# The product W3·Wout inside a fused attention and MoE kernel: third matrix loaded transposed, contraction outside, four row blocks in four banks, the last unit's sums in one piece

## The chip, the cores and the metric

One core of one Trainium2 chip runs the whole program. The metric is the device time of one execution in microseconds; the time before is a median of three runs. Engines are named as the profile names them: PE (TensorE, with PEld for its weight loads), DVE (VectorE), ACT (ScalarE), POOL (GpSimd), SP (SyncE, which issues nearly all DMAs).

## The reference

```python
def _attn_ref(q, k, v, w1, b1, w2):            # 8 batches, 8 heads, 576 positions, 64 wide
   scores = q @ k^T / 8 + bias(i, j)           # bias: a small MLP of the relative position
   attn = exp(scores - max) / sum
   return attn @ v

def _moe_ref(x, w1, w2, w3, w_out):            # x: 4608 x 512; w1, w2: 512 x 1024
   a = x @ w1
   b = x @ w2
   h = a * b @ w3                              # w3: 1024 x 1024
   return (h @ w_out).astype(np.float32)       # w_out: 1024 x 512
```

`x` is the attention's output, 4608 tokens by 512. The four MoE matrices arrive as 64-bit floats.

## The kernel before

**Two stages with a seam.** The attention runs over 32 units (4 pairs of heads by 8 batches). Then the MoE part runs over 9 chunks of 512 tokens. Between them lies the seam, which the change is about: the kernel uses (a·b)·W3·Wout = (a·b)·(W3·Wout), so it computes the 1024 x 512 product W3·Wout once ("folding") and the MoE stage needs only `up` (both products with w1 and w2) and `down` (one product with the folded matrix).

**Order.** Every step of every engine has a planned time, in microseconds of the plan: `arrange` writes those of the attention, `put` and `put_w` those of the seam and the MoE part. `drive` hands the steps over in the order of the planned times, and the program is then built from them; PE, DVE, ACT and POOL each run their instructions strictly in the order in which they stand there. The order rows below show what was built. The plan's times are no measured times.

**One attention unit.** S: scores, 9 row tiles named `0246M1357`, each into one of two 2-bank buffers `ps_s`. T (DVE): adds the bias `nb` and finds the row minimum `mx`. E (ACT): the exponentials, into `pp`, with row sums into `sums`. R (DVE): transposes a pair of tiles into `pt`. W0 to W7 (PE, line 352): the products of `pt` with v, all into `acc`, four banks. X (ACT): copies `acc` into `x`, which goes to DRAM as `x_d`. Step `r` inverts the row sums and sends them out. A unit's W pieces stand among the S of the unit behind it; the last unit has none behind it.

**64-bit weights.** A matrix piece of 128 x 512 is fetched as 512 KB into `wi`, of which there are two buffers, and turned into 32-bit floats by two ACT, four DVE and two POOL steps (`narrow`, lines 140 to 164): `wmag` and the low part on ACT, clamp on POOL or DVE, shift, head and power on DVE, two POOL steps for the total. The 24 pieces of w3 and w_out are done during the attention, in `wos` and `w3s`. The 16 pieces of w1 and w2 are done in the seam and during the first `up` steps (`split_w`, clamps on DVE); the fetch of a piece waits until POOL has done with the piece two before it.

**Two-part numbers.** Each factor of a product is split into a high part (ACT, names with h) and a low part, the difference (DVE or POOL, names with l), and three PE matmuls are issued for each product: high·high, high·low, low·high.

**The seam before.** `split_wo(i)` splits the 8 row blocks of w_out: `woh` on ACT, `wol` on POOL (even i) or DVE (odd i). `fold(ft, hf)`, 16 calls, goes over the 8 row blocks ft of w3 and the two halves of its columns: 4 PE transposes into `w3t` (line 561), `w3h` on ACT (565) and `w3l` on DVE (567), both out of PSUM, then 12 matmuls of 128 x 512 into `wacc` (573), which holds one row block of the result. After the second half, two steps put the high and the low part of that row block into SBUF (579 on ACT, 581 on DVE). Buffers for `w3h` and `w3l`: two each. `w3t` takes one bank, `wacc` two banks in turn.

**The MoE stage.** `up(c, ft)`: 24 matmuls (614), then a, g, gh, gl on ACT and DVE. `down(c, ft)`: 12 matmuls (639) into four accumulators, one step behind. PE order at the start: up, up, down, up, down, and so on. The tokens of a chunk are loaded as `xr`, multiplied by the inverted sums `rb`, and split into `xh` (POOL) and `xl` (DVE).

Of the kernel before, what the change touches and what calls it, by code (L numbers as in the profile page):

```python
# [78 lines left out]
def relpos_attention_moe(  # L79
# [477 lines left out]
    def fold(ft, hf):  # L557
        ts = range(hf * NF // 2, (hf + 1) * NF // 2)
        tp = pst.tile([P, NF // 2, P], F32, name="w3t")
        for n, t in enumerate(ts):  # L560
            nc.tensor.transpose(tp[:, n], w3s[ft][:, t * P:(t + 1) * P], ident)  # L561
        yield
        w3h = fp.tile([P, NF // 2, P], F32R, name="w3h")
        w3l = fp.tile([P, NF // 2, P], F32R, name="w3l")
        nc.scalar.activation(w3h, tp, AF.Copy)
        yield
        nc.vector.tensor_tensor(w3l, tp, f(w3h), op=ALU.subtract)
        yield
        if hf == 0:
            wacc[ft] = psw.tile([P, DO], F32, name="wacc")  # L570
        for n, t in enumerate(ts):
            for m, (l, r) in enumerate(((w3h, woh), (w3h, wol), (w3l, woh))):
                nc.tensor.matmul(  # L573
                    wacc[ft], l[:, n], r[t], start=(t == 0 and m == 0), stop=(t == NF - 1 and m == 2),
                )
        yield
        if hf == 1:
            w = held.tile([P, 2, DO], F32R, name=f"w3s{ft}")
            nc.scalar.activation(w[:, 0], wacc[ft], AF.Copy)
            yield  # L580
            nc.vector.tensor_tensor(w[:, 1], wacc[ft], f(w[:, 0]), op=ALU.subtract)
            folded[ft] = w
# [48 lines left out]
    def down(c, ft):  # L631
        d = chunks[c]
        gh, gl = d["g"].pop(ft)
        for t in range(NT):
# [3 lines left out]
            for n, (l, r) in enumerate(((gh, 0), (gh, 1), (gl, 0))):  # L638
                nc.tensor.matmul(  # L639
                    d["o", t], l[:, sl], folded[ft][:, r],  # L640
# [11 lines left out]
    for i in range(NF):  # L652
        put(later, split_wo(i), t_s + AT_WO + i * PACE_WO, t_s + AT_WO + i * PACE_WO + 0.8)
    for i in range(2 * NF):
        at = t_s + AT_F + min(i, N_F) * PACE_F0 + max(i - N_F, 0) * PACE_F
        put(later, fold(*divmod(i, 2)), *(at + d for d in AT_FOLD))
    for t in range(2):
        for m in range(2):
            put_w(later, w01, t, m, t_s + AT_W1 + PACE_W * (2 * t + m))
# [84 lines left out]
```

## Time and profile before

| | |
|---|---|
| time before, median of 3 runs | 1181.52 us (1175.22 to 1184.53) |
| the profiled execution | 1180.03 us, span 1178.2 us, granted PE clock 0.981 |
| busy | PE 1112.6, PEld 771.2, DVE 686.3, ACT 484.1, POOL 181.2 us |
| last score tile's reduction starts (DVE, line 270) | 513.25 us |
| first and last fold matmul start (PE, line 573) | 519.5 and 584.7 us |
| first `down` matmul starts (PE, line 639) | 594.5 us |

The seam lies between 513 and 595 us. A line with "idle before" says how long the engine waited ahead of its instructions and what ended that wait. Line numbers are those of the kernel before.

### The profile page before, as it was taken

What the parts mean: (1) busy time and instruction counts of PE and PEld (TensorE: products, weight loads), DVE (VectorE), ACT (ScalarE), POOL (GpSimd) and SP (SyncE); (2) the same over time, 40 slices, a digit from 0 to 9 for tenths busy, and PEclk for the clock granted to TensorE, in tenths of its full rate; (3) what the DMA queues carried; (4) which work ended last, traced back from release to release, by engine and by line L of the source; (5) the groups of instructions that cost most, each with busy time, mean ns of one, the idle gap of its engine ahead of it and who ended that gap; (6) DMA issues with size and microseconds to landing.
All of it is one profiled execution on the core that took longest, in us unless ns stands there. A gap on an engine that the chain in (4) does not pass through costs nothing.

```text
span 1178.2 us, 34156 instructions
## 1 busy us (share of the span) xinstructions
PE 1112.6 (94%) x14720; PEld 771.2 (65%) x14720; DVE 686.3 (58%) x1284; ACT 484.1 (41%) x1071; POOL 181.2 (15%) x152
## 2 busy tenths in 40 slices
PE   7769989998899999898999999999999999999998
PEld 3225445444444554466888888888888888888887
DVE  8779988998899999986885222223131222223111
ACT  6756655665566666664442212121211212121212
POOL 0003320321033123333543000000000000000000
PEclk9979999999999999998999999999999999999999
DMA  8887786767776766636431211202010211100000
GB/s 261 279 261 229 231 285 206 242 214 244 234 234 222 237 222 205 217 120 173 132 117 54 72 36 54 54 36 72 35 55 19 72 36 56 52 36 1 36 1 36
DMA packets 91959, 158.51 MB, mean 135 GB/s; under 512 B 18336, under 2 KB 32800, under 8 KB 91808
## 3 DMA queue, kind: packets, MB, share of 16 engines
q1 hardware_dynamic: 91376, 156.31, 41.6%
q8 instruction: 115, 1.88, 0.6%
q14 instruction: 36, 0.29, 0.1%
q10 hardware_dynamic: 432, 0.02, 0.0%
HBM read 126.36 MB, written 29.92 MB: 133 GB/s over the span
## 4 chain that ended last, share of the span: by engine, by line
PE 68%; DVE 19%; issue 5%; DMA 5%; ACT 2%; SPq 0%; DVEq 0%; POOL 0%; ACTq 0%; POOLq 0%
PE up L614 33%; PE o L639 17%; PE acc L352 8%; DVE ts L270 8%; DVE pt L309 7%; PE s L259 6%; PE wacc L573 3%; DMA nb_d<-bev 2%; DMA v<-in_v_dram 1%; PE bacc L473 1%; DVE wmag L155 1%; ACT pp L299 1%; DVE wi L160 1%; DVE zdve L459 1%; PE w3t L561 0%
## 5 line engine op out<-in xcount | busy, mean ns | idle before, releaser
L352 PE MATMUL acc<-pt,v 32*64 32x128 f32 (+1 forms) x9216 | 245.0, 298 | 21.9 <-issue 12.2
L352 PEld LDWEIGHTS acc<-pt,v 32*64 32x64 f32 x9216 | 158.2, 133 | 145.0 <-issue 110.7
L622 DVE TENSOR_TENSOR g<-up,a 128x512 f32<-128x512 f32 x72 | 49.8, 691 | 342.8 <-PE up L614 342.8
L299 ACT ACTIVATE pp<-ts,mx 128x576 f32<-128x576 f32 x256 | 196.5, 769 | 95.0 <-DVE mx L270 93.9
L259 PE MATMUL s<-k,q 64*64 64x288 f32 x2304 | 208.8, 442 | 21.2 <-DVE mx L270 16.0
L614 PE MATMUL up<-xl,wh 128*128 128x512 f32 x576 | 225.1, 391 | 0.0
L614 PE MATMUL up<-xh,wl 128*128 128x512 f32 x576 | 225.1, 391 | 0.0
L614 PE MATMUL up<-xh,wh 128*128 128x512 f32 x576 | 225.1, 391 | 0.0
L270 DVE CUSTOM_DVE_ANT_0 ts<-s,nb 128x576 f32<-128x576 f32 x256 | 184.9, 745 | 41.1 <-PE s L259 28.2
L639 PE MATMUL o<-w3s,gh 128*128 128x512 f32 x576 | 177.7, 390 | 0.0
L309 DVE STREAM_TRANSPOSE pt<-pp 128x1152 f32<-128x1152 f32 x128 | 175.5, 1371 | 0.1
L619 ACT COPY a<-up 128x512 f32<-128x512 f32 x72 | 42.3, 587 | 257.7 <-PE up L614 257.7
L259 PEld LDWEIGHTS s<-k,q 64*64 64x64 f32 x2304 | 63.3, 135 | 97.8 <-issue 48.1
L614 PEld LDWEIGHTS up<-xh,wl 128*128 128x128 f32 x576 | 108.2, 188 | 23.4
L614 PEld LDWEIGHTS up<-xl,wh 128*128 128x128 f32 x576 | 108.2, 188 | 23.4
L614 PEld LDWEIGHTS up<-xh,wh 128*128 128x128 f32 x576 | 108.2, 188 | 23.3
L639 PEld LDWEIGHTS o<-w3s,gh 128*128 128x128 f32 x576 | 108.1, 188 | 22.9
L625 ACT ACTIVATE gh<-g 128x512 fp32r<-128x512 f32 x72 | 45.5, 633 | 178.3 <-DVE g L622 178.3
L639 PE MATMUL o<-w3s,gl 128*128 128x512 f32 x288 | 112.1, 389 | 0.0
L600 POOL TENSOR_SCALAR xh<-xr 128x512 fp32r<-128x512 f32 x36 | 23.2, 645 | 443.3 <-DVE xr L596 443.3
L628 DVE TENSOR_TENSOR gl<-g,gh 128x512 fp32r<-128x512 f32 x72 | 51.6, 717 | 50.7 <-ACT gh L625 50.5
L146 POOL TENSOR_SCALAR wmag<-wmag 128x512 f32<-128x512 f32 x24 | 46.0, 1915 | 207.9 <-ACT wmag L140 174.0
(67 smaller groups left out, 937.3 us busy)
## 6 DMA issues: line engine op xcount, KB each, us to landing
v<-in_v_dram SPq DMA_DIRECT2D x64, 320.0 KB
k<-in_k_dram SPq DMA_DIRECT2D x64, 288.0 KB
q<-in_q_dram SPq DMA_DIRECT2D x64, 288.0 KB
v<-in_v_dram SPq DMA_DIRECT2D x64, 256.0 KB
wi<-in_moe_w_dram SPq DMA_DIRECT2D x32, 512.0 KB
nb_d<-bev SPq DMA_DIRECT2D x36, 295.5 KB
nb<-nb_d SPq DMA_DIRECT2D x16, 576.0 KB
x_d<-x SPq DMA_DIRECT2D x32, 288.0 KB
```

The source lines that it names most:

```text
L146: clamps.tensor_scalar(d["mag"], d["mag"], LEAST, MOST, op0=ALU.max, op1=ALU.min)
L259: nc.tensor.matmul(s[outs, hf, :HS], d[f"q{h}"][rows, q0:q0 + 64], d[f"k{h}"][rows, hf * HS:(hf + 1) * HS], start=True, stop=True,)
L270: nc.vector.tensor_tensor_reduce(out=halves(ts), in0=d.pop(("s", t))[:, :, :HS], in1=halves(NB[p, t]), op0=ALU.add, op1=ALU.min, scale=-1. ...
L299: nc.scalar.activation(d["p", ps][:, k * S:(k + 1) * S], ts, AF.Exp, bias=mx, scale=-1.0, accum_out=SUMS[u // 4 % 2][:, col:col + 1],)
L309: nc.vector.transpose(o, st[u].pop(("p", ts)))
L352: nc.tensor.matmul(acc[outs, a, c0:c0 + 32 * (t1 - t0)], d["v", b][rows, h], pt_[rows, t0:t1, 32 * b:32 * b + 32], start=(b == 0), stop=(b ...
L614: nc.tensor.matmul(acc, l[:, cc], r, start=(n == 0), stop=(n == 3 * NC - 1))
L619: nc.scalar.copy(a, ps[0])
L622: nc.vector.tensor_tensor(g, ps[1], a, op=ALU.mult)
L625: nc.scalar.activation(gh, g, AF.Copy)
L628: nc.vector.tensor_tensor(gl, g, f(gh), op=ALU.subtract)
L639: nc.tensor.matmul(d["o", t], l[:, sl], folded[ft][:, r], start=(ft == 0 and n == 0), stop=(ft == NF - 1 and n == 2),)
```

## The change

- w3 is handed over transposed by the host, so its pieces are already what `fold` needs as left factor. The PE transposes, their bank and the identity matrix go away. `w3h` and `w3l` are made from the SBUF tiles `w3s` (now 16 half tiles).
- The loops of `fold` are swapped: the contraction block t is outside. A call `fold(t, hf)` issues the same 12 matmuls, 3 for each of four row blocks, into four accumulators `wacc0` to `wacc3`. The first four row blocks (hf = 0) use the banks of the score buffers `ps_s`, the other four those of `acc`. The high and low parts of the result (`keep`) come in two groups of four, after t = 7 of each half.
- `split_wo(t)` goes along with `fold(t, 0)`.
- The last unit's W0 to W7 stand together, behind its last R and behind the first two folds. Its X moves with them.
- The seam begins earlier in the plan (behind the last T, not the last E), and the planned paces change: folds 2.74 instead of 3.04, weight pieces 5.5 instead of 6.56, the tokens of chunk 0 at 20.0 instead of 30.68. `ps_ab`, the banks of `up`, moves to the other side of PSUM.

```diff
+AT_F, PACE_F, AT_SUMS, LEN_SUMS = 1.9, 2.74, 5.4, 5.5
+AT_EV, PACE_EV = 0.4, 1.25
+AT_W1, PACE_W, AT_X, PACE_X = 6.0, 5.5, 20.0, 2.10
...
+    last = {}
+    for n in range(len(PARTS)):
+        last[f"W{n}"] = at["R57"][0] + 1.4 + 0.62 * n, "PE"
+    last["X"] = last["W7"][0] + 0.9, "ACT"
...
-    t_s = max(e[0] for e in later if e[3][0] in "SE") + 0.5
+    t_s = max(e[0] for e in later if e[3][0] in "ST") + 0.05
...
-            nc.tensor.transpose(tp[:, n], w3s[ft][:, t * P:(t + 1) * P], ident)
...
+    def split_w3(t, hf):
+        h = fp.tile([P, DO], F32R, name="w3h")
+        l = fp.tile([P, DO], F32R, name="w3l")
+        w3[t, hf] = (h, l)
+        nc.scalar.activation(h, w3s[t][hf], AF.Copy)
+        yield
+        nc.vector.tensor_tensor(l, w3s[t][hf], f(h), op=ALU.subtract)
+
+    def fold(t, hf):
+        h, l = w3.pop((t, hf))
+        for k in range(NF // 2):
+            ft = hf * NF // 2 + k
+            if t == 0:
+                wacc[ft] = psw[hf].tile([P, DO], F32, name=f"wacc{k}")
+            cs = slice(k * P, (k + 1) * P)
+            for m, (a, r) in enumerate(((h, woh), (h, wol), (l, woh))):
                 nc.tensor.matmul(
+                    wacc[ft], a[:, cs], r[t], start=(t == 0 and m == 0), stop=(t == NF - 1 and m == 2),
                 )
...
+    t_f = t_s + AT_F
     for i in range(2 * NF):
+        hf, t = divmod(i, NF)
+        at, t_f = t_f, t_f + PACE_F + (LEN_SUMS if i == 1 else 0.0)
+        put(later, fold(t, hf), at)
+        put(later, split_w3(t, hf), at - 2.2, at - 1.0)
+        if hf == 0:
+            put(later, split_wo(t), at - 2.1, at - 1.9)
...
+    inputs["moe_w3"] = inputs["moe_w3"].T
```

The order moves at three places that the prediction speaks of. First, **DVE around the last unit's last transposes** (`pp_9208` holds tiles 1 and 3, `pp_9265` or `pp_9297` tiles 5 and 7; the two ISA rows with `ts` are T5 and T7). Before:

```order
L270 ISA ts_9259,mx_9260<-s_9203,nb5_6594 128x576
L270 ISA mx_9260 128x1
L270 ISA ts_9262,mx_9263<-s_9235,nb5_6594 128x576
L270 ISA mx_9263 128x1
L309 STREAM_TRANSPOSE pt1_839<-pp_9208 128x1152
L316 TENSOR_SCALAR sums1_117<-sums1_117 128x36
L317 RECIPROCAL sums1_117<-sums1_117 128x36
L319 STREAM_TRANSPOSE rt_9348<-sums1_117 128x64
L309 STREAM_TRANSPOSE pt1_839<-pp_9265 128x1152
L555 TENSOR_TENSOR wos0_9380<-wos1_77,woh1_9321 128x512
L567 TENSOR_TENSOR w3l_9396<-w3t_9341,w3h_9395 128x512
```

The same place on DVE in the changed kernel:

```order
L311 STREAM_TRANSPOSE pt1_839<-pp_9208 128x1152
L272 ISA ts_9259,mx_9260<-s_9203,nb5_6594 128x576
L272 ISA mx_9260 128x1
L272 ISA ts_9262,mx_9263<-s_9235,nb5_6594 128x576
L272 ISA mx_9263 128x1
L563 TENSOR_TENSOR w3l_9293<-w3s0_0_60,w3h_9292 128x512
L555 TENSOR_TENSOR wos0_9365<-wos1_77,woh1_9282 128x512
L318 TENSOR_SCALAR sums1_117<-sums1_117 128x36
L319 RECIPROCAL sums1_117<-sums1_117 128x36
L321 STREAM_TRANSPOSE rt_9369<-sums1_117 128x64
L311 STREAM_TRANSPOSE pt1_839<-pp_9297 128x1152
L563 TENSOR_TENSOR w3l_9357<-w3s1_0_62,w3h_9356 128x512
```

The transpose of tiles 1 and 3 moved ahead of T5 and T7; the low part `wos0` (wol of block 1), which needs `woh1` of ACT, moved ahead of the last transpose.

Second, **ACT at the same place**: the two exponentials of tiles 5 and 7, and X of the unit before the last (`x_9334`, `x_9336`). Before:

```order
L299 ACTIVATE pp_9265,sums1_117<-ts_9259,mx_9260 128x576
L299 ACTIVATE pp_9265,sums1_117<-ts_9262,mx_9263 128x576
L550 ACTIVATE woh0_9320<-wos0_76 128x512
L361 ACTIVATE x_9334<-acc_9089 128x4x4x32
L366 ACTIVATE x_9334<-acc_9089 64x64 x2
L550 ACTIVATE woh1_9321<-wos1_77 128x512
L550 ACTIVATE woh2_9322<-wos2_78 128x512
L565 ACTIVATE w3h_9395<-w3t_9341 128x512
```

In the changed kernel:

```order
L561 ACTIVATE w3h_9292<-w3s0_0_60 128x512
L550 ACTIVATE woh0_9281<-wos0_76 128x512
L301 ACTIVATE pp_9297,sums1_117<-ts_9259,mx_9260 128x576
L301 ACTIVATE pp_9297,sums1_117<-ts_9262,mx_9263 128x576
L363 ACTIVATE x_9336<-acc_9089 128x4x4x32
L368 ACTIVATE x_9336<-acc_9089 64x64 x2
L561 ACTIVATE w3h_9356<-w3s1_0_62 128x512
L550 ACTIVATE woh1_9282<-wos1_77 128x512
```

The first `w3h` and `woh` moved ahead of the two exponentials. In the built program that `w3h` waits for the end of T7 (`mx_9263`), since its tile lies in memory that the attention's loads and bias rows held until then.

Third, **PE within the folds**, one call each. Before, with the transposes of the next call ahead of it:

```order
L561 MATMUL w3t_9675<-ident_60,w3s2_70 128x128 x4
L573 MATMUL wacc_9659<-woh4_9324,w3h_9656 128x512
L573 MATMUL wacc_9659<-wos3_9453,w3h_9656 128x512
L573 MATMUL wacc_9659<-woh4_9324,w3l_9657 128x512
L573 MATMUL wacc_9659<-woh5_9325,w3h_9656 128x512
L573 MATMUL wacc_9659<-wos4_9478,w3h_9656 128x512
L573 MATMUL wacc_9659<-woh5_9325,w3l_9657 128x512
```

In the changed kernel, the first call behind the last unit's sums:

```order
L354 MATMUL acc_9397<-pt1_839,v3_9334 64x160
L573 MATMUL wacc0_9340<-woh2_9283,w3h_9555 128x512
L573 MATMUL wacc0_9340<-wos1_9560,w3h_9555 128x512
L573 MATMUL wacc0_9340<-woh2_9283,w3l_9556 128x512
L573 MATMUL wacc1_9344<-woh2_9283,w3h_9555 128x512
L573 MATMUL wacc1_9344<-wos1_9560,w3h_9555 128x512
```

The transposes are gone, and the third matmul of a call already needs the low part `w3l`, which it also did before.

More of the change, by code (lines that the diff above doesn't have):

```diff
@@ L184, in relpos_attention_moe @@
     held = ctx.enter_context(tc.tile_pool(name="held", bufs=1))
-    w3s = [held.tile([P, DF], F32, name=f"w3s{t}") for t in range(NF)]
+    w3s = [[held.tile([P, DO], F32, name=f"w3s{t}_{hf}") for hf in range(2)] for t in range(NF)]
     wos = [held.tile([P, DO], F32, name=f"wos{t}") for t in range(NF)]
@@ L555, in split_wo, with keep @@
         eng.tensor_tensor(wol[i], wos[i], f(woh[i]), op=ALU.subtract)
[L557 to L561, printed above, removed]
-        yield
[L563 to L572, printed above, removed]
+    def split_w3(t, hf):
[3 more added lines that the diff above has]
+        nc.scalar.activation(h, w3s[t][hf], AF.Copy)
+        yield
+        nc.vector.tensor_tensor(l, w3s[t][hf], f(h), op=ALU.subtract)
[7 more added lines that the diff above has]
+            for m, (a, r) in enumerate(((h, woh), (h, wol), (l, woh))):
                 nc.tensor.matmul(
-                    wacc[ft], l[:, n], r[t], start=(t == 0 and m == 0), stop=(t == NF - 1 and m == 2),
+                    wacc[ft], a[:, cs], r[t], start=(t == 0 and m == 0), stop=(t == NF - 1 and m == 2),
                 )
         yield
[L577 to L582, printed above, removed]
+    def keep(ft):
+        hf, k = divmod(ft, NF // 2)
+        h, l = [held.tile([P, DO], F32R, name=f"w3s{2 * k + i}_{hf}") for i in range(2)]
+        nc.scalar.activation(h, wacc[ft], AF.Copy)
+        yield
+        nc.vector.tensor_tensor(l, wacc[ft], f(h), op=ALU.subtract)
+        folded[ft] = (h, l)
     def load_x(c):
@@ L649, in down @@
                 yield
[L652 to L653 removed]
+    t_f = t_s + AT_F
     for i in range(2 * NF):
[L655 to L659, printed above, removed]
+        hf, t = divmod(i, NF)
[4 more added lines that the diff above has]
+            put(later, split_wo(t), at - 2.1, at - 1.9)
+        if t == NF - 1:
+            for k in range(NF // 2):
+                put(later, keep(hf * NF // 2 + k), t_f + AT_EV + k * PACE_EV, t_f + AT_EV + k * PACE_EV + 0.6)
+            if hf == 0:
+                t_h = t_f + AT_EV + 3 * PACE_EV + 0.61
+    for n in range(4):
+        put_w(later, w01, n // 2, n % 2, t_s + AT_W1 + PACE_W * n)
     drive([e for e in later if e[0] <= end])
@@ L674, in relpos_attention_moe @@
     fo.close()
+    ps_ab = moe.enter_context(tc.tile_pool(name="ps_ab", bufs=2, space=PSUM, side="right"))
     gp = moe.enter_context(tc.tile_pool(name="gp", bufs=2))
```

29 lines of the change are left out of this document (11 added, 18 removed).

## The prediction

> **What bounds the kernel now.** I read the page first (busy times, then the chain that ended last), then the seam: stretches of time, the chain in order of time, and single instructions.
>
> ```profile
> PE 1112.6 (94%) x14720; PEld 771.2 (65%) x14720; DVE 686.3 (58%) x1284; ACT 484.1 (41%) x1071; POOL 181.2 (15%) x152
> PE up L614 33%; PE o L639 17%; PE acc L352 8%; DVE ts L270 8%; DVE pt L309 7%; PE s L259 6%; PE wacc L573 3%; DMA nb_d<-bev 2%; DMA v<-in_v_dram 1%; PE bacc L473 1%; DVE wmag L155 1%; ACT pp L299 1%; DVE wi L160 1%; DVE zdve L459 1%; PE w3t L561 0%
> ```
>
> PE is busy for 94% of the span and `up` and `down` make half of the chain. The change leaves those alone, so everything is decided between the last score tile and the first `down`. The next rows are stretches: from and to, length, busy time (and count) of PE, PEld, DVE, ACT and POOL, the granted PE clock, the DMA share and GB/s.
>
> ```profile
> 517.00:531.00 14.00, 12.87 (x318) 9.94 (x318) 9.96 (x13) 7.21 (x14) 7.07 (x5) 1.00 0.39 119
> 535.00:540.00 5.00, 5.00 (x15) 3.84 (x15) 1.88 (x4) 1.74 (x3) 2.63 (x2) 0.54 0.97 226
> 533.25:580.57 47.32, 45.12 (x209) 36.38 (x210) 38.54 (x60) 20.81 (x37) 20.01 (x17) 0.93 0.54 153
> 566.00:585.10 19.10, 19.10 (x93) 15.67 (x94) 18.08 (x27) 10.20 (x18) 8.71 (x7) 1.00 0.48 151
> 595.00:650.00 55.00, 55.00 (x244) 45.47 (x243) 36.68 (x52) 18.71 (x31) 20.79 (x17) 1.00 0.28 86
> ```
>
> In the last third of the seam (566 to 585.10) PE is busy all the time, and so the transposes there stand on the path. But DVE is busy 18.08 of the same 19.10 us: **two engines are at their limit side by side**, and the change takes work from only one of them. In the middle (535 to 540) the clock was 0.54. The chain shows the pieces of a fold there:
>
> ```profile
> 535.10 4.91 PE wacc L573 x12
> 540.01 0.44 PE w3t L561 x4
> 540.45 2.79 PE wacc L573 x12
> 585.10 9.60 PE up L614 x41
> 594.70 2.73 PE o L639 x12
> ```
>
> A call of `fold` costs 2.79 us of matmuls (0.233 each) and 0.44 of transposes; with the low clock 4.91. The last rows give `up`: 41 matmuls in 9.60 us, 0.234 each, and the first `down` at 594.70. Seven of the 48 matmuls of the first two `up` were done earlier, between folds.
>
> **What goes from PE.** 16 calls by 0.44 us are 7.0 us of transposes. PE's waits within the folds could go too, the longest being 3.75 us, which the low clock followed:
>
> ```profile
> 533.99 1.11 PE L561 MATMUL w3t<-ident,w3s 128*128 128x128 f32 x4 [3.75 <-DVE w3l L567]
> 483.25 0.71 PE L259 MATMUL s<-k,q 64*64 64x288 f32 x8 [2.47 <-DVE mx L270]
> 480.00:490.00 10.00, 7.53 (x240) 4.27 (x243) 7.99 (x17) 4.79 (x11) 0.77 (x2) 1.00 0.66 232
> ```
>
> The second row is a wait of 2.47 us in the attention; the clock stayed at 1.00 there (third row).
>
> **The start of the seam, step by step.** Rows of DVE, ACT, POOL and PE: start, duration, instruction, and in brackets the wait before it.
>
> ```profile
> 513.25 0.76 DVE ts L270
> 513.93 1.37 DVE L309 STREAM_TRANSPOSE pt<-pp 128x1152 f32<-128x1152 f32 x1
> 515.22 0.14 DVE L316 TENSOR_SCALAR sums<-sums 128x36 f32<-128x36 f32 x1
> 515.98 1.33 DVE L309 STREAM_TRANSPOSE pt<-pp 128x1152 f32<-128x1152 f32 x1
> 514.04 0.78 ACT L299 ACTIVATE pp<-ts,mx 128x576 f32<-128x576 f32 x1 [0.43 <-DVE mx L270]
> 515.46 0.60 ACT L361 ACTIVATE x<-acc 128x512 f32<-128x512 f32 x1
> 516.41 1.15 ACT L550 ACTIVATE woh<-wos 128x512 fp32r<-128x512 f32 x2
> 515.51 1.27 POOL L555 TENSOR_TENSOR wol<-wos,woh 128x512 fp32r<-128x512 f32 x1 [10.00 <-ACT woh L550]
> 513.00 1.91 PE L352 MATMUL acc<-pt,v 32*64 32x160 f32 x96
> L352 PE MATMUL acc<-pt,v 32*64 32x128 f32 (+1 forms) x9216 | 245.0, 298 | 21.9 <-issue 12.2
> ```
>
> Before, T7 ended at 514.01 and the last transpose (R57) began at 515.98. Now the transpose of tiles 1 and 3 (1.37) stands ahead of T5 and T7, into a wait of 0.60: T7 ends 0.77 later, at 514.8. The first `w3h` waits for that, and behind it on ACT are queued `woh` (1.15 for the pair, from the row of two), the two exponentials (0.78 each), X of the unit before (0.95, from 515.46 to 516.41), and the second `w3h` and `woh` (1.15): 514.8 + 1.15 + 1.56 + 0.95 + 1.15 = 519.6. This is **the added wait**: `wos0` on DVE needs that `woh` and stands ahead of the sums (0.76, from 515.22 to 515.98) and of R57 (1.33). So R57 ends at 519.6 + 0.68 + 0.76 + 1.33 = 522.4, where before it ended at 517.3. PE fills part of this with the first fold. The second fold stalls at its third matmul until `w3l` behind R57 is there (0.68, 523.1), then needs 10 matmuls (2.3): 525.4. The last unit's sums are 9216 / 32 = 288 records; 96 took 1.91 us, so 5.7: 531.1. Then X (0.95) and the third `w3h` (0.6), and the third `w3l` can begin at **532.7**. Before:
>
> ```profile
> 533.25 0.68 DVE L567 TENSOR_TENSOR w3l<-w3t,w3h 128x512 fp32r<-128x512 f32 x1
> 580.57 0.68 DVE L567 TENSOR_TENSOR w3l<-w3t,w3h 128x512 fp32r<-128x512 f32 x1
> ```
>
> The third `w3l` began at 533.25 and the sixteenth at 580.57. So the rearranged start gives back only 0.55 us, and at the third `w3l` both kernels have 14 folds ahead of them.
>
> **The rest of the seam.** PE then has 14 times 2.79 = 39.1 us of matmuls, DVE needs more: in those 47.32 us before, it was busy 38.54 and idle 8.78. By the built order the new stretch has 62 DVE instructions instead of 59: three more low parts of w_out (L555), one more clamp and shift (L146, L149), and two fewer low parts of the result (L581), since the last four come after the folds.
>
> ```profile
> L555 DVE TENSOR_TENSOR wos<-wos,woh 128x512 fp32r<-128x512 f32 x4 | 2.7, 679 | 1.6 <-POOL wos L555 1.6
> L581 DVE TENSOR_TENSOR w3s<-wacc,w3s 128x512 fp32r<-128x512 f32 x8 | 5.5, 688 | 2.7 <-ACT w3s L579 2.7
> 519.97 0.42 DVE L146 TENSOR_SCALAR wmag<-wmag 128x512 f32<-128x512 f32 x1
> 520.42 0.43 DVE L149 TENSOR_SCALAR wmag<-wmag 128x512 int32<-128x512 int32 x1
> ```
>
> That is 3 x 0.68 + 0.42 + 0.43 - 2 x 0.69 = 1.5, so 40.05. The tokens' and the pieces' work is the same. What isn't the same is **where `w3l` reads**. Pairs of POOL and DVE rows at one time:
>
> ```profile
> 563.44 1.29 POOL L163 TENSOR_TENSOR w<-w,wi 128x512 f32<-128x512 f32 x1
> 563.50 1.78 DVE xl L602
> 535.61 1.29 POOL L163 TENSOR_TENSOR w<-w,wi 128x512 f32<-128x512 f32 x1 [5.09 <-issue]
> 535.77 0.69 DVE L567 TENSOR_TENSOR w3l<-w3t,w3h 128x512 fp32r<-128x512 f32 x1 [0.30 <-ACT w3h L565]
> 580.19 1.30 POOL L163 TENSOR_TENSOR w<-w,wi 128x512 f32<-128x512 f32 x1 [1.14 <-ACT w3s L579]
> ```
>
> `xl`, with both inputs in SBUF, began 0.06 behind a POOL instruction and took 1.78 us; it was over some 0.55 after POOL was. `w3l` out of PSUM at 535.77 and 580.57 ran its 0.69 and 0.68 beside POOL as if it were not there. Seven of the 14 started inside a POOL instruction, the two shown being the first and the last. Now `w3l` reads `w3s` and `w3h`, both in SBUF. Bounds: nothing, if it behaves like L555, also with two SBUF inputs, whose mean is 0.68; at most 1.1 each (1.78 less 0.68), 7.7 for seven. I take 0.6 each, **4.2 us**: what ran for free beside POOL now has to follow it, but the next instruction, which would have waited instead, then doesn't.
>
> [...]
>
> Three `wol` on POOL (1.27 each) now fall into the stretch too: between nothing and 3.8 us of blocked DVE, I take half, 1.9. DVE's idle time: before 8.78, half of it in the cold stretch, now between nothing and as much; since DVE always has a queue when PE has none, I take 2. Sum: 40.05 + 4.2 + 1.9 + 2 = 48.15. The last `w3l` begins at 532.7 + 48.15 = 580.85, against 580.57. Then 0.68, 10 matmuls (2.33), and all 48 matmuls of `up` (11.24): first `down` at **595.1, against 594.7: 0.4 us later**.
>
> **At no cost, and the cover.** The last four results (`keep`, 0.69 on DVE each) hide under the first two `up`, 11.24 us; uncovered they would cost 2.8. The other bank side for `up` is free after the eighth fold, long before. The pieces of w1 and w2 come at 5.5 instead of 6.56 in the plan, but by the order as many stand ahead of the last `w3l` as before; later, from 595 to 650, DVE was busy only 36.68 of 55. On SP's queue the token loads stand behind a wait for the last sums (531.1); their first use is three calls later on DVE, so some 10 us; a miss would be idle time of DVE and lies in its bounds. The matrix pieces in the attention keep size and count.
>
> **The rivals.**
> - **PE sets the pace.** DVE keeps up, if POOL blocks little. The third fold's second matmul waits for `wol` on POOL: 532.65 + 0.58 + 1.27 = 534.5. 14 x 2.79 = 39.1 lead to 573.6, `up` to 584.8: 9.9 us earlier, 1170.1 in the profile's measure. For it: the 7.0 us and the cold stretch go. Against: DVE would have to do 40 us of own work and all of POOL's 20 us in 41.
> - **The clock falls in the waits (slower).** If DVE sets the pace, each fold waits for `w3l`; DVE's pace is 48.15 / 14 = 3.4 us a fold. One fold at the low clock takes 4.91, so 2.12 more, and is then slower than DVE. It decides from waits between 2.47 us (clock kept) and 3.75 us (clock lost). The third fold waits 2.2 us and again 1.3; where the eight token instructions stand between the `w3l` of folds 5 to 9, waits of 3 to 4 us are possible. Six cold folds: 12.7 us more, 1193.1. Against: evenly spread, a fold waits only 0.6.
>
> [...]
>
> **How the numbers follow.** The profiled execution took 1180.03; the median shown is 1181.52, 1.5 above, with runs from 1175 to 1185, so about 1% is what can be told from no change. Forecast 1180.4, on the median's scale **1182**, with its own range 1176 to 1191 (6 below if blocking and idle time come out low, 9 above if both come out high): chance 0.62. PE's pace 0.20, at 1171.6. The clock 0.12, at 1194.6. The remaining 0.06 is spread. The first two hold 0.82, so the range is 1170 to 1191. Faster by over 1% needs 11.8 us, more than PE's pace gives: 0.07. Slower by over 1%: most of the clock's and a little of the forecast's, 0.13. Within: 0.80.
>
> **What would show it.** Right: R57 ends near 522, the third `w3l` near 533, the last near 581; `w3l` has a mean well over 0.68; PE's busy share from 535 to 580 is below one, its waits ended by `w3l`. Wrong: folds follow each other at 2.79 (PE's pace), or at 4.9 with a clock near 0.5 (the other rival). I'd also be wrong if R57 didn't wait for `wos0`.

## The result, and the profile after

| | before | after |
|---|---|---|
| median time | 1179.34 us (1169.46 to 1184.53, 20 runs) | 1187.29 us (1178.34 to 1194.01, 20 runs) |
| ratio, 95% interval | | **1.0066** (1.0046 to 1.0085) |
| span of the profiled execution | 1178.2 us | 1181.3 us |

The changed kernel is slower by 0.66%, 7.8 us (5.4 to 10.0), in an interval that excludes no change. The forecast was "no change" at 1182 us. The time lies in the range and within 1%, but the forecast put 0.4 us where 7.8 were measured. The two profiled executions below show 5.7 us of this between the attention and the first `down`; for the rest no place is shown.

The page after: busy times, and the chain that ended last.

```profile
PE 1108.4 (94%) x14656; PEld 765.1 (65%) x14656; DVE 695.4 (59%) x1284; ACT 484.8 (41%) x1071; POOL 183.1 (16%) x150
PE up L616 33%; PE o L641 17%; DVE ts L272 8%; PE acc L354 8%; DVE pt L311 7%; PE s L261 6%; DMA nb_d<-bev 3%; ACT pp L301 1%; PE wacc L573 1%; DVE wmag L157 1%; ACT bev L480 1%; DMA wi<-in_moe_w_dram 1%; DVE wi L162 1%; ACT bev L481 1%; DMA nbM<-nb_d 1%
```

DVE's busy time rose by 9.1 us though it has as many instructions (1284), and PE's fell by 4.2. To compare single executions, I count from the first matmul of the last score tile to the first `down`, since the attention ahead of it differs from run to run. The first fence is PE's rows before, the second PE's rows after; the third is the chain after, in order of time.

```profile
512.35 0.72 PE L259 MATMUL s<-k,q 64*64 64x288 f32 x8
594.54 0.63 PE L639 MATMUL o<-w3s,gh 128*128 128x512 f32 x2
```

```profile
509.63 0.71 PE L261 MATMUL s<-k,q 64*64 64x288 f32 x8
523.17 3.78 PE L354 MATMUL acc<-pt,v 32*64 32x160 f32 x205
528.57 1.84 PE L354 MATMUL acc<-pt,v 32*64 32x128 f32 x83 [1.62 <-issue]
597.55 0.63 PE L641 MATMUL o<-w3s,gh 128*128 128x512 f32 x2
```

```profile
581.08 5.38 PE wacc L573 x22
586.47 11.24 PE up L616 x48
```

Before, this took 594.54 - 512.35 = 82.2 us, after, 597.55 - 509.63 = **87.9**. What follows takes 583.7 us in both (1178.2 - 594.54 and 1181.3 - 597.55). The next fence has DVE's rows after, at four marks: the last transpose R57, the third `w3l`, the first product of the tokens with the inverted sums (`xr`, with the instruction behind it), and the sixteenth `w3l`. The row below them is the `xr` of the kernel before.

```profile
518.69 1.33 DVE L311 STREAM_TRANSPOSE pt<-pp 128x1152 f32<-128x1152 f32 x1
532.07 0.69 DVE L563 TENSOR_TENSOR w3l<-w3s,w3h 128x512 fp32r<-128x512 f32 x1 [9.41 <-ACT w3h L561]
542.72 0.68 DVE L598 TENSOR_TENSOR xr<-xr,rb 128x512 f32<-128x512 f32 x1
543.32 0.68 DVE L563 TENSOR_TENSOR w3l<-w3s,w3h 128x512 fp32r<-128x512 f32 x1
582.07 0.69 DVE L563 TENSOR_TENSOR w3l<-w3s,w3h 128x512 fp32r<-128x512 f32 x1
```

```profile
551.57 0.68 DVE L596 TENSOR_TENSOR xr<-xr,rb 128x512 f32<-128x512 f32 x1
```

Counted from the last score tile, with the prediction's steps counted from 512.35:

| | before | predicted | after |
|---|---|---|---|
| R57 ends | 5.0 | 10.05 | 10.4 |
| last unit's sums end | 17.3 | 18.75 | **20.8** |
| third `w3l` begins | 20.9 | 20.35 | **22.4** |
| first `xr` product | 39.2 | | 33.1 |
| sixteenth `w3l` begins | 68.2 | 68.5 | **72.4** |
| first `down` | 82.2 | 82.6 | **87.9** |

Three terms were too small: the start by 2.1 us (third `w3l`), the stretch to the last `w3l` by 1.85 (50.0 against 48.15), the tail by 1.4; together 5.3. The next rows are stretches (columns as in the prediction). Before, from the first `xr` product to the last `w3l`:

```profile
551.57:580.57 29.00, 27.54 (x135) 21.98 (x134) 27.01 (x40) 12.66 (x23) 14.64 (x13) 1.00 0.47 145
```

After, from the third `w3l` to the first `xr` product, and from there to the last `w3l`:

```profile
532.07:542.72 10.65, 9.26 (x38) 7.05 (x38) 8.99 (x13) 6.24 (x12) 5.29 (x4) 1.00 0.87 229
542.72:582.07 39.35, 30.14 (x113) 21.57 (x113) 38.53 (x51) 17.95 (x31) 20.12 (x15) 0.96 0.41 131
```

From the first `xr` product on, **DVE is busy for 38.53 of 39.35 us**; PE is busy for 30.14, so it waits. Where the DVE time went is seen in the groups of DVE instructions between the third and the sixteenth `w3l` (count, busy time, mean ns of one). Before:

```profile
L567 DVE TENSOR_TENSOR w3l<-w3t,w3h 128x512 fp32r<-128x512 f32 x13 | 8.9, 683 | 5.4 <-ACT w3h L565 5.4
L146 DVE TENSOR_SCALAR wmag<-wmag 128x512 f32<-128x512 f32 x6 | 3.5, 582 | 1.4 <-ACT wmag L140 1.4
L149 DVE TENSOR_SCALAR wmag<-wmag 128x512 int32<-128x512 int32 x6 | 4.5, 747 | 0.1
```

After:

```profile
L563 DVE TENSOR_TENSOR w3l<-w3s,w3h 128x512 fp32r<-128x512 f32 x13 | 10.3, 795 | 9.4 <-ACT w3h L561 9.4
L148 DVE TENSOR_SCALAR wmag<-wmag 128x512 f32<-128x512 f32 x7 | 9.0, 1293 | 1.0 <-ACT wmag L142 0.9
L151 DVE TENSOR_SCALAR wmag<-wmag 128x512 int32<-128x512 int32 x7 | 6.3, 893 | 0.1
```

The clamp and the shift take 0.42 and 0.43 us undisturbed (the rows at 519.97 and 520.42 of the prediction). Now their means are 1.29 and 0.89. A POOL row and a DVE row show one case: the shift began 0.24 us behind the start of a POOL step and ended 0.28 us behind that step's end.

```profile
573.53 1.36 POOL L166 TENSOR_TENSOR w<-wmag,w 128x512 f32<-128x512 f32 x1
573.77 1.40 DVE L151 TENSOR_SCALAR wmag<-wmag 128x512 int32<-128x512 int32 x1
```

Taking every DVE row of the stretch at more than its undisturbed length (0.42 for clamp, shift and power, 0.68 for the others), the excess was 6.9 us before (POOL busy 20.0) and is **15.1 us** after (POOL busy 25.4): clamp 6.1, shift 3.3, `xl` 2.2, `w3l` 1.5, `wol` 1.1, the rest 0.9.

The start times of the two traces say where all of it comes from. After, 19 DVE instructions of the stretch start while a POOL instruction runs. The one that reads PSUM (a low part of the result) keeps its length. Each of the other 18 takes longer by what was left of the POOL instruction, less 0.12 to 0.15 us, and these 18 make 15.0 of the 15.1 us. Before, 17 start inside a POOL instruction: seven of them read PSUM (six `w3l`, one low part of the result) and keep their length, one meets the last 0.04 us of it, and the nine others make 6.7 of the 6.9 us.

### The profile page after: what moved, and what is told of

Read it like the earlier page. It is cut to its first block, busy times and chain, and to the rows that moved or that the text cites. A ratio compares the mean times of both kernels' runs of the same rounds, so it can differ in the third digit from the quotient of the medians.

```text
span 1181.3 us, 34030 instructions
## 1 busy us (share of the span) xinstructions
PE 1108.4 (94%) x14656; PEld 765.1 (65%) x14656; DVE 695.4 (59%) x1284; ACT 484.8 (41%) x1071; POOL 183.1 (16%) x150
## 4 chain that ended last, share of the span: by engine, by line
PE 65%; DVE 18%; issue 6%; DMA 6%; ACT 4%; SPq 1%; POOL 0%; DVEq 0%; ACTq 0%
PE up L616 33%; PE o L641 17%; DVE ts L272 8%; PE acc L354 8%; DVE pt L311 7%; PE s L261 6%; DMA nb_d<-bev 3%; ACT pp L301 1%; PE wacc L573 1%; DVE wmag L157 1%; ACT bev L480 1%; DMA wi<-in_moe_w_dram 1%; DVE wi L162 1%; ACT bev L481 1%; DMA nbM<-nb_d 1%
## 5 line engine op out<-in xcount | busy, mean ns | idle before, releaser
L354 PE MATMUL acc<-pt,v 32*64 32x160 f32 (+1 forms) x9216 | 242.4, 298 | 18.5 <-issue 10.1
L272 DVE CUSTOM_DVE_ANT_0 ts<-s,nb 128x576 f32<-128x576 f32 x256 | 185.1, 746 | 37.8 <-PE s L261 22.9
L616 PEld LDWEIGHTS up<-xh,wl 128*128 128x128 f32 x576 | 108.2, 188 | 23.3
L616 PEld LDWEIGHTS up<-xh,wh 128*128 128x128 f32 x576 | 108.2, 188 | 23.3
```

The source lines that it names most:

```text
L272: nc.vector.tensor_tensor_reduce(out=halves(ts), in0=d.pop(("s", t))[:, :, :HS], in1=halves(NB[p, t]), op0=ALU.add, op1=ALU.min, scale=-1. ...
L354: nc.tensor.matmul(acc[outs, a, c0:c0 + 32 * (t1 - t0)], d["v", b][rows, h], pt_[rows, t0:t1, 32 * b:32 * b + 32], start=(b == 0), stop=(b ...
L616: nc.tensor.matmul(acc, l[:, cc], r, start=(n == 0), stop=(n == 3 * NC - 1))
```

## The experiments

Times are ratios to the kernel before, with their 95% intervals; each variant ran 10 or 12 times, against 17 to 31 runs of the kernel before. Marks are counted from the last score tile, in one profiled execution each. Single executions of one kernel differ by several us (the changed kernel's took 1178 to 1194), so verdicts on the time go by the ratio, and the marks show only where time moved in one execution.

| run | ratio | sums end | third `w3l` | first `xr` | last `w3l` | first `down` |
|---|---|---|---|---|---|---|
| before | 1 | 17.3 | 20.9 | 39.2 | 68.2 | 82.2 |
| changed kernel | 1.0066 (1.0046 to 1.0085) | 20.8 | 22.4 | 33.1 | 72.4 | 87.9 |
| e1 before, `w3l` from SBUF | 1.0032 (1.0005 to 1.0059) | 17.3 | 20.9 | 39.5 | 70.4 | 84.9 |
| e2 no POOL steps | 0.9985 (0.9961 to 1.0008) | 22.9 | 24.6 | 35.5 | 67.0 | 83.2 |
| e3 `wos0` late | 1.0065 (1.0039 to 1.0090) | 17.9 | 19.5 | 32.3 | 71.7 | 88.7 |
| e4 early splits | 1.0036 (1.0007 to 1.0065) | 23.3 | 12.3 | 33.9 | 73.2 | 90.2 |
| e5 slow pieces | 1.0075 (1.0049 to 1.0101) | 20.8 | 22.4 | 33.4 | 69.6 | 85.7 |
| e6 PE filled | 1.0051 (1.0023 to 1.0079) | 21.8 | 23.5 | 36.3 | 75.7 | 92.4 |
| e7 `wos0` late, PE warm | 1.0033 (1.0005 to 1.0060) | 18.2 | 19.8 | 30.5 | 69.8 | 86.9 |
| e8 sums apart | 1.0022 (0.9995 to 1.0048) | 21.0 | 12.0 | 28.5 | 68.1 | 83.6 |
| e9 POOL's work on DVE, ACT | 1.0027 (1.0000 to 1.0053) | 19.0 | 20.7 | 37.7 | 71.3 | 86.1 |
| e10 sums apart, X late | 1.0006 (0.9982 to 1.0031) | 21.0 | 12.1 | 27.2 | 66.6 | 83.7 |
| e11 before, PE warm | 0.9996 (0.9967 to 1.0025) | 17.3 | 20.9 | 39.5 | 68.6 | 82.4 |
| e12 e10 with e9 | **0.9964** (0.9936 to 0.9992) | 19.6 | 11.0 | 25.8 | 63.2 | 78.3 |

**e1: only the source of `w3l`, in the kernel before.**

```diff
-        nc.vector.tensor_tensor(w3l, tp, f(w3h), op=ALU.subtract)
+        nc.vector.tensor_tensor(w3l, w3s[ft].rearrange("p (a b c) -> p a b c", a=2, b=NF // 2)[:, hf], f(w3h), op=ALU.subtract)
```

> The kernel before; only the first source of w3l is the SBUF tile w3s in place of the PSUM tile w3t (its values are then wrong; length and order are the same). Theory A, my 4.2 us: w3l out of SBUF collides with POOL, where out of PSUM it did not. Then the mean of w3l rises from 0.68 to 0.8 or more, the time that DVE instructions take beyond their undisturbed length between the third and the sixteenth w3l rises from 6.9 us by 2 to 8, and since DVE has 8.5 us of idle time in this stretch, the first down comes 1 to 4 us later, counted from the last score tile (82.2 us in the kernel before). Rival: the source does not matter, w3l keeps 0.68, the stretch stays at 47.3 us and the first down within 0.5 us.

Theory A held. The group of `w3l` in the same stretch as above (0.68 before):

```profile
L567 DVE TENSOR_TENSOR w3l<-w3s,w3h 128x512 fp32r<-128x512 f32 x13 | 11.5, 881 | 2.6 <-ACT w3h L565 2.6
```

The excess rose from 6.9 to 10.2 us, the stretch from 47.3 to 49.5, the first `down` came 2.7 us later. So in the kernel before, the source of `w3l` alone is worth 2.2 us of the stretch, not the 4.2 that I took.

**e2: without POOL's two steps per piece** (w1 and w2 then lack their high parts).

```diff
-        steps = [fetch, size, rest, clamp, shift, head, power, total]
+        steps = [fetch, size, rest, clamp, shift, head, power, total if pieces == 1 else lambda: None]
```

> The changed kernel without the two POOL steps (total) of the pieces of w1 and w2, so that these matrices lack their high parts. Theory A, POOL and DVE in each other's way set the pace of the folds: the time beyond the undisturbed length falls from 15.1 us to 4 or less, third to sixteenth w3l from 50.0 to 40 us (36.6 of own work, some 3 of the rest), and the first down comes 8 to 11 us earlier, counted from the last score tile (87.9 us). Rival, the pieces' chain of fetches and steps sets the pace, or the high parts on ACT: DVE shows idle time in place of the collisions, and the stretch stays above 46 us.

From the first `xr` product to the last `w3l`:

```profile
546.90:578.41 31.51, 28.66 (x115) 22.17 (x114) 29.15 (x51) 17.41 (x31) 5.34 (x5) 0.95 0.55 158
```

31.5 us instead of 39.4, with the same DVE instructions; the excess between third and sixteenth `w3l` fell from 15.1 to 4.7. From the third `w3l` on, the stretch came to 42.5, not 40, since 3.0 us of idle time lay ahead of `xr`. The sums also ended 2.1 us later, and the first `down` came 4.7 us earlier, not 8 to 11. The time fell below the changed kernel's by 0.8% (the intervals are apart). Theory A held in kind, not in size; the rival is out.

**e3 and e7: the added wait.** `wos0` goes behind the last transpose; in e7, PE also runs eight matmuls of zeros ahead of the third fold.

```diff
-            put(later, split_wo(t), at - 2.1, at - 1.9)
+            put(later, split_wo(t), at - 2.1, at - 1.9 + (0.95 if t == 1 else 0.0))
```

```diff
         h, l = w3.pop((t, hf))
+        for n in range((8 if (t, hf) == (2, 0) else 0) if t else 0):       # e7 only
+            nc.tensor.matmul(wacc[hf * NF // 2], zero[:, 0:P], zero, start=False, stop=False)
```

> The changed kernel with wos0 on DVE behind the last transpose R57 and behind the second w3l. Theory B, the added wait costs what I priced: R57 begins when the second exponential is through, about 515.5 to 516 instead of 518.7 on the clock of the profile after, the second fold ends about 2 us earlier, and so do the last unit's sums, the third w3l and the first down: 85.5 to 86.5 us from the last score tile instead of 87.9. Rival: the second fold waits for wos0 instead, the sums end less than 0.7 us earlier and the first down does not move.

> As the run with wos0 behind the last transpose, and with eight matmuls of zeros (1.9 us) on PE between the last unit's sums and the third fold, where PE stood idle and then ran at 0.55 to 0.60 of its clock for some 8 us. Theory: the 2.9 us that the earlier transpose gained at the third w3l were lost to the low clock. Then the third fold runs at full clock, and the first down comes at 85 to 86.5 us from the last score tile instead of 88.7 without the filling (87.9 in the changed kernel). Rival, DVE's queue behind the third w3l takes as long anyway: 87.5 to 88.7.

In e3 the sums ended 2.9 us earlier and the third `w3l` began 2.9 earlier, as theory B has it, but the first `down` came 0.8 us later instead of 1.4 to 2.4 earlier. Two stretches behind the third `w3l`, e3 first, then e7:

```profile
531.68:535.68 4.00, 3.11 (x7) 2.27 (x8) 4.00 (x7) 1.59 (x4) 1.28 (x1) 0.55 0.94 177
535.68:539.68 4.00, 4.00 (x12) 3.10 (x12) 1.58 (x4) 1.89 (x4) 0.67 (x1) 0.60 0.88 251
```

```profile
527.58:531.58 4.00, 2.99 (x12) 2.09 (x12) 4.00 (x6) 1.86 (x4) 1.28 (x1) 1.00 0.90 225
531.58:535.58 4.00, 4.00 (x19) 3.26 (x18) 2.75 (x5) 3.12 (x6) 2.45 (x2) 1.00 0.92 249
```

At a clock of 0.55 and 0.60, PE finished the third fold late, and with it came the buffer that the fifth `w3h` waited for (ACT idle 4.5 us). In e7 the clock was 1.00 and the first `xr` product came at 30.5 instead of 32.3; the first `down` came at 86.9, just short of the 85 to 86.5 expected. So the added wait is real in the profiles. In the times, taking it away shows nothing in e3 and 0.3% in e7, where the intervals overlap: its worth is unclear.

**e4: splits of calls 2 and 3 earlier**, ahead of X on ACT.

```diff
+        e = 3.0 if i in (2, 3) else 0.0
-        put(later, split_w3(t, hf), at - 2.2, at - 1.0)
+        put(later, split_w3(t, hf), at - 2.2 - e, at - 1.0 - e)
-            put(later, split_wo(t), at - 2.1, at - 1.9)
+            put(later, split_wo(t), at - 2.1 - e, at - 1.9 - e)
```

> The changed kernel with the splits of calls 2 and 3 (w3h, w3l, woh, wol) planned 3 us earlier: the third w3h and woh then stand on ACT ahead of the last unit's X, and the third w3l on DVE directly behind the first weight piece. Theory C: the 9.4 us for which DVE waits for the third w3h, because ACT has X in front of it, are what the changed start loses. Third w3l about 8 us earlier, third fold at the end of the sums, 3 to 4 us of DVE work out of the crowded stretch: first down 3 to 5 us earlier (83 to 85 us from the last score tile instead of 87.9). Rival: the wait moves to the next instruction (the piece's clamp behind its fetch, or the tokens, whose loads stand behind X's DMA), and the first down moves by less than 1 us.

The expectation failed. The third `w3l` came 10 us earlier, but a POOL step moved ahead too, the second `w3l` collided with it (1.27 us), and the second fold stood still at a low clock. The wait was longer than in the changed kernel (0.86), so the sums ended 2.6 us and the first `down` 2.3 us later:

```profile
526.87 0.80 PE L573 MATMUL wacc<-woh,w3l 128*128 128x512 f32 x1 [2.75 <-DVE w3l L563]
```

```profile
525.21:531.21 6.00, 4.34 (x10) 3.14 (x10) 4.01 (x7) 1.27 (x2) 2.78 (x3) 0.57 0.17 56
```

The median is 0.3% below the changed kernel's, with intervals that overlap: unclear.

**e5: two pieces fewer in the stretch.**

```diff
-AT_W1, PACE_W, AT_X, PACE_X = 6.0, 5.5, 20.0, 2.10
+AT_W1, PACE_W, AT_X, PACE_X = 6.0, 8.0, 20.0, 2.10
+PACE_L = 4.8
...
-        at = t_s + AT_W1 + PACE_W * n
+        at = t_s + AT_W1 + PACE_W * min(n, 5) + PACE_L * max(n - 5, 0)
```

> The changed kernel with the pieces of w1 and w2 planned every 8.0 us up to the sixth and every 4.8 us after it, instead of every 5.5: by the built order five pieces instead of seven stand on DVE between the third and the sixteenth w3l. Theory A, DVE with its collisions is the pace: two pieces fewer are 2 x 2.6 us of own DVE work (0.42, 0.41, 0.68, 0.41, 0.68) and about two sevenths of the pieces' part of the 15.1 us of collisions, together 8 to 9 us, so that the stretch falls from 50.0 to 41 to 43 us, near PE's 39.1, and the first down comes 6 to 8 us earlier counted from the last score tile (80 to 82 us instead of 87.9); the two pieces move under the first up and down, where DVE had 14 of 55 us free, and the whole is 5 to 7 us faster than the changed kernel. Rival, the start (waits and clock) holds it: the stretch keeps 48 us or more. Second rival: the late pieces stop the first up steps, and the gain in the seam is lost again behind it.

The expected gain failed and the second rival came true. The stretch fell to 47.1 us, not to 41 to 43: the excess fell to 10.6, but DVE was idle for 7.7. The first `down` came 2.2 us earlier, but PE then stopped for pieces and for `gl`, in the stretches from 20 to 60 us behind it:

```profile
614.92:634.92 20.00, 18.93 (x81) 14.56 (x79) 17.63 (x24) 7.47 (x14) 10.52 (x8) 1.00 0.43 131
634.92:654.92 20.00, 18.21 (x75) 13.92 (x76) 10.38 (x16) 6.04 (x11) 5.93 (x4) 1.00 0.09 27
```

PE was busy for 18.93 and 18.21 of 20 us there, and in the changed kernel for 20.00 of each. At this pace the late pieces come when `up` already waits for them, and PE lost 2.9 us again.

**e6: two more matmuls per call for PE** (zeros as in e7, two ahead of every call but the first of each half; the text below says "but the two first"; the 14 calls are right).

> The changed kernel with two more matmuls of 128x512 (zeros times zeros, into the same accumulator) ahead of every call of fold but the two first: 14 x 2 x 0.233 = 6.5 us more for PE, as much as the removed transposes took. Theory A, PE has slack in every call and the 7 us of transposes were not on the path any more: the first down moves by less than 1.5 us (87.9), or comes a little earlier if PE keeps its clock better. Rival, PE is the pace in most calls: 5 to 6.5 us later.

From the first `xr` product to the last `w3l` PE was busy for 33.85 us instead of 30.14, and that stretch did not grow: 39.4 us.

```profile
547.71:587.15 39.44, 33.85 (x135) 25.79 (x134) 38.59 (x52) 18.07 (x31) 20.35 (x15) 0.96 0.40 125
```

The first `down` of the profiled execution was later by 4.5 us, between what the theory and the rival expected; 3.2 of them lie ahead of that stretch, 1.0 up to the third `w3l` and 2.2 from there to the first `xr` product. The median is not above the changed kernel's (1.0051 against 1.0066); the intervals leave room for under 4 us, not for 6.5. So in the changed kernel 6.5 us of matmuls on PE cost no time that can be told. Whether the transposes were as free in the kernel before, no run shows: there they stand on the chain in the last third of the seam.

**e8 and e10: the last unit's sums apart again.** In e10, X of the last unit also stands 2.0 later in the plan.

```diff
-    for n in range(len(PARTS)):
-        last[f"W{n}"] = at["R57"][0] + 1.4 + 0.62 * n, "PE"
-    last["X"] = last["W7"][0] + 0.9, "ACT"
-    last["xd"] = last["X"][0] + 0.8, "SP"
+    last["X"] = at["X"][0] + 2.0, "ACT"                   # e10 only
+    last["xd"] = last["X"][0] + 0.8, "SP"                 # e10 only
...
-        at, t_f = t_f, t_f + PACE_F + (LEN_SUMS if i == 1 else 0.0)
+        at, t_f = t_f, t_f + PACE_F + (LEN_SUMS / 2 if i < 2 else 0.0)
```

> The changed kernel with one part undone: the last unit's sums stand apart among the first three folds, as in the kernel before, and its X where it was. Theory C, the start lost 2 us because X and with it the third w3h wait for the whole block of sums (DVE idle for 9.4 us): the third w3l comes 3 to 5 us earlier than 22.4 us from the last score tile, and the first down 2 to 4 us earlier than 87.9. Rival, DVE's pace in the crowded stretch holds what the start gains, since the same 62 instructions stand there: first down within 1 us of 87.9.

> As the run with the last unit's sums apart (83.6 us from the last score tile to the first down), and X of the last unit 2.0 us later in the plan, behind the fifth w3h and woh and the first wh on ACT. There DVE waited 5.5 us for wh, which stood behind X. Theory C, in-order waits for the sums are what the start loses: that wait falls below 3 us, first down at 80.5 to 82.5, at or under the 82.2 of the kernel before, and the time within 0.3% of the kernel before. Rival, DVE's later queue takes it back: 83 to 84.

Among the runs that undo a part of the change, none gave as much: 1.0066 became 1.0022 (the intervals just touch), then 1.0006 (apart). R57 and the first `xr` product in e8:

```profile
524.18 1.33 DVE L307 STREAM_TRANSPOSE pt<-pp 128x1152 f32<-128x1152 f32 x1
546.37 0.68 DVE L594 TENSOR_TENSOR xr<-xr,rb 128x512 f32<-128x512 f32 x1
```

The sums ended no earlier (21.0 in both, against 20.8), but folds ran between them, and DVE used the time: the first `xr` product came 4.6 and 5.9 us earlier. (In the new plan `wos0` also fell behind R57, which began at 6.3 instead of 9.1; e3 shows what that alone is worth.) In e10 the first `down` did not come earlier than in e8 in the profiled execution, as its rival had it: the last `w3l` came 1.5 us earlier, but from there to the first `down` it took 17.1 us instead of 15.5.

**e11: the cold stretch of the kernel before.**

```diff
+        if (ft, hf) == (1, 1):
+            warm = psf.tile([P, DO], F32, name="warm")
+            for n in range(14):
+                nc.tensor.matmul(warm, zero[:, 0:P], zero, start=True, stop=True)
         tp = pst.tile([P, NF // 2, P], F32, name="w3t")
```

> The kernel before with 14 matmuls of zeros (3.3 us) on PE ahead of the fourth fold's transposes, where PE stood idle for 3.75 us and then ran at 0.54 of its clock from 534 to 540. Theory, the cold stretch costs PE 2.8 us (6.0 us at 0.54) and PE is the pace there: clock 1.00 from then on, first down 2 to 3 us earlier than 82.2 from the last score tile, time 0.2% less. Rival, DVE is the pace behind it in the kernel before too: first down moves by less than 1 us, and the removal of this stretch, which the change promised, was worth little from the first.

The rival held. The clock was 1.00 where it had been 0.54, and the first `down` stayed (82.4). What was won ahead of it was lost again where ACT waited for a piece's fetch, which came no earlier (34.3 us from the last score tile against 33.8):

```profile
532.80:536.80 4.00, 4.00 (x21) 3.27 (x20) 2.62 (x5) 1.19 (x3) 1.91 (x2) 1.00 0.83 217
```

```profile
543.07 0.66 ACT L140 ACTIVATE wmag<-wi 128x512 f32<-128x512 f32 x1 [4.83 <-DMA wi<-in_moe_w_dram]
```

**e9 and e12: POOL out of the seam, nothing left out.** e9 on the changed kernel, e12 on e10.

```diff
         def total():
-            nc.gpsimd.tensor_tensor(x, x, f(d["power"]), op=ALU.mult)
-            nc.gpsimd.tensor_tensor(x, d["mag"], x, op=ALU.add)
+            eng = nc.gpsimd if pieces == 1 else nc.vector
+            eng.tensor_tensor(x, x, f(d["power"]), op=ALU.mult)
+            eng.tensor_tensor(x, d["mag"], x, op=ALU.add)
...
-        eng = nc.vector if i % 2 else nc.gpsimd
+        eng = nc.vector
...
-        nc.gpsimd.tensor_scalar(xh, xr, 1.0, 1.0, op0=ALU.mult, op1=ALU.mult)
+        nc.scalar.activation(xh, xr, AF.Copy)
```

> The changed kernel with nothing left out, but with POOL's work of the seam and the MoE part given away: the two total steps of the pieces and all wol on DVE, xh on ACT. Theory A, collisions with POOL are what DVE loses: DVE gets 14 x 0.60 + 3 x 0.60 = 10.2 us more between the third and the sixteenth w3l (instructions that follow each other undisturbed start 0.60 us apart), but the 15.1 us beyond the undisturbed lengths go, so that the stretch falls from 50.0 to 45 to 48 us and the first down comes 2 to 5 us earlier than 87.9 us from the last score tile. Rival, busy times simply add up and the collisions are only apparent: the stretch grows to 56 us or more, the first down comes 6 us later or worse.

> The changed kernel with both edits that shortened it: the last unit's sums apart with X 2.0 us later (first token product on DVE at 27.2 us from the last score tile, but 39.4 us from there to the last w3l), and POOL's work of the seam and the MoE part on DVE and ACT (33.6 us from there to the last w3l, but a late start). Theory A: the two add up, first token product at 27 to 29.5, last w3l at 61 to 63, first down at 75.5 to 78 instead of 82.2 in the kernel before, and the time 4 to 6 us (0.3 to 0.5%) under the kernel before. Rival: what DVE has to do behind the first down (it was busy 19.3 of 20 us there) stops the up and down steps, and the gain is lost there; or the third piece's fetch behind the tokens' loads holds the start again: first down at 81 or later.

From the first `xr` product to the last `w3l`, e9 and e12:

```profile
544.42:578.03 33.61, 31.13 (x116) 22.81 (x117) 31.82 (x59) 19.76 (x36) 0.00 (x0) 0.91 0.47 138
```

```profile
542.69:580.11 37.42, 29.98 (x115) 22.88 (x115) 31.92 (x58) 19.97 (x35) 0.00 (x0) 0.91 0.57 164
```

In e9, DVE did 58 instructions instead of 50 in 33.6 us instead of 39.4: the excess was 0.3 us. The start lost most of it, since the first `total` now stood behind the sums on DVE and the third piece's fetch behind the tokens' loads (ACT waited 7.4 us for it). From the third `w3l` on, the stretch took 50.6 us, 8.9 of them idle, where 45 to 48 were expected, and the first `down` came only 1.8 us earlier. In e12 the start was early as well, and the first `down` came at 78.3 (75.5 to 78 expected), though DVE was idle for 5.3 us, most of it again behind a fetch. It is 0.36% (0.08 to 0.64) **faster than the kernel before**, and about 1% under the changed one. This does not set the change itself in the right: what POOL's work on DVE and ACT would give in the kernel before, no run shows.

## Why the prediction was right and wrong

- **Right: DVE is the pace of the second part.** From the first `xr` product to the last `w3l`, every variant with POOL's and the pieces' work in place took 39.3 to 39.6 us, however early it began and whatever PE had to do (changed kernel, e3, e4, e6, e7, e8, e10). As much matmul time as the transposes took, put back, costs nothing that can be told (e6), and the cold stretch of the kernel before, taken away there, brings nothing (e11). The rival "PE sets the pace" fell.
- **Right: the start up to the second fold.** R57 10.4 against 10.05, second fold's end 13.6 against 13.05, 62 DVE instructions and 2.1 us of idle time in the stretch against 62 and 2.
- **Wrong: the sums.** I priced them at 5.7 us from their rate; they took 7.2. PE stood still for 1.62 us between two of them (row at 528.57), for which the profile shows no releaser. From the second `w3l` to the third, with the block of sums between them, 12.1 us went by here and 11.5 to 14.3 in e2, e3, e5, e6, e7 and e9, whose sums stand in one block too; without the hole it would have been 10.5 here (an estimate, 12.1 less 1.62). In the kernel before and in e12, where folds stand between the sums, every wait among the last unit's sums has a releaser. My guess for the hole is PE's supply of instructions. The profile has a DMA queue that it calls "instruction" (packets, MB, share of the DMA engines):

```profile
q8 instruction: 115, 1.88, 0.6%
```

That is 16 KB a packet, and 64 bytes for each of PE's 29312 matmuls and weight loads if the queue carries these alone, or one packet for 128 matmuls (an estimate from these counts). Before the hole, 205 matmuls took 3.78 us, so by this estimate the sums use up a packet in 2.4 us; folds, at 2.79 us for 12 matmuls, take 30. In the trace such a packet ended at 527.28, and PE went on at 528.57, 1.29 us behind it. No run changed the supply, so the cause of the hole is not shown.
- **Wrong in kind: what the block of sums does to the rest.** I counted it only as a delay of the third `w3l`. It also leaves DVE idle for 9.4 us ahead of that `w3l` (its row above) while other DVE work stood behind it in the queue. With the sums apart (e8), DVE comes to the first `xr` product 4.6 us earlier, and everything behind follows: by the ratios 0.44 of the 0.66%, with the earlier R57 of that plan in it.
- **Mis-sized: the collisions.** To the 6.9 us that were in the old busy time I added 4.2 for `w3l` and 1.9 for `wol`: 13.0. Measured: 15.1. The place was wrong as well: of the 8.2 us more, 6.5 fell on clamp and shift, 1.5 on `w3l`, 1.1 on `wol`, and the rest shrank by 0.9. POOL's 20 us before ran in part beside DVE's idle time (8.8 us) and beside `w3l` out of PSUM; now DVE is nearly always busy, and 18 of the 19 instructions that start inside a POOL instruction read SBUF alone and wait. I priced the effect for `w3l`, which reads two tensors; the clamp reads one, all seven of the stretch began inside a POOL instruction, and they took 0.92 to 1.51 us, 1.29 in the mean, beside 0.42 undisturbed.
- **Wrong: the tail.** I let 10 matmuls (2.33 us) follow the last `w3l`. The last two `w3l` began 1.7 us apart, since a clamp and a shift, both held up by POOL, stood ahead of the fifteenth:

```profile
577.79 1.23 DVE L148 TENSOR_SCALAR wmag<-wmag 128x512 f32<-128x512 f32 x1 [0.48 <-ACT wmag L142]
579.05 1.37 DVE L151 TENSOR_SCALAR wmag<-wmag 128x512 int32<-128x512 int32 x1
580.35 0.68 DVE L563 TENSOR_TENSOR w3l<-w3s,w3h 128x512 fp32r<-128x512 f32 x1
```

From the fifteenth on 22 matmuls were left (5.38 us in the chain above). When the sixteenth ended (582.76), PE had 3.7 us of them before it, so `up` began 1.4 us later than I had put it.
- **The clock** fell, but not as its rival had it: no row of six cold folds, only single stretches. The rival's price did not follow either: at a pace of 3.4 us a fold, a fold of 4.91 costs 1.5 us, not 2.12, and six of them 9.1. And the condition was wrong. I let it decide between waits of 2.47 and 3.75 us. The same two waits of PE, 1.42 and 0.85 us ahead of the first two matmuls of the folds, were followed by a clock of 0.72 in the changed kernel (first fence) and 1.00 in e3 (second), 4 to 10 us behind the last score tile in both:

```profile
513.61 0.51 PE L573 MATMUL wacc<-woh,w3h 128*128 128x512 f32 x1 [1.42 <-ACT woh L550]
514.96 0.69 PE L573 MATMUL wacc<-wol,w3h 128*128 128x512 f32 x1 [0.85 <-POOL wol L555]
513.63:519.63 6.00, 5.15 (x14) 3.67 (x14) 2.40 (x6) 4.67 (x11) 1.27 (x1) 0.72 0.90 275
```

```profile
515.66 0.49 PE L573 MATMUL wacc<-woh,w3h 128*128 128x512 f32 x1 [1.42 <-ACT woh L550]
517.01 0.50 PE L573 MATMUL wacc<-wol,w3h 128*128 128x512 f32 x1 [0.85 <-POOL wol L555]
515.68:521.68 6.00, 4.65 (x18) 3.33 (x19) 4.52 (x10) 4.65 (x11) 1.27 (x1) 1.00 0.83 255
```

One order of PE's program and the same two waits had two outcomes, so what decides the clock is not shown.

## What to carry to other kernels

Before taking work off one engine, ask which engine is busy to the brim in that stretch, and sum its time as it is with its neighbours at work, not as its undisturbed instructions add up. The collisions with POOL fell here on whatever DVE instruction reading SBUF alone happened to start inside a POOL instruction (18 in the changed kernel, 15.0 us), so the mean of one kind of instruction tells little; take the excess of all. And a long block on one engine, with an in-order instruction behind it that others need, costs the idle time of those others (DVE's 9.41 us ahead of the third `w3l`): here breaking the block up gave time back (1.0066 became 1.0022 in e8), while 6.5 us of added PE work, nearly as much as the transposes had taken, left no mark on the time that can be told.
